# One order for all engines, worked out by a pass in time inside the kernel, for a convolution attention with two feed-forward layers

## The chip, the cores and the metric

The kernel runs on one core of a Trainium2 chip. The metric is the device time of one execution in microseconds (us), the median of three runs.

## What is computed

`x` and `weight_gen` are float32, the four weight matrices float64, taken in as pairs of 32-bit words. Products are made in fp32r with split operands (a high part and a low part).

```python
# x (2, 4096, 192), weight_gen (2, 4096, 8, 7)
w = softmax(weight_gen, axis=-1)                 # over the 7 taps, per token and head
x = einsum('bshk,bskhg->bshg', w, windows of 7 rows of x, zeros before the first)
x = x.reshape(8192, 192)
h = x @ w_in1;  x = (h * cos(h)) @ w_out1        # w_in 192 x 2048, w_out 2048 x 192
h = x @ w_in2;  x = maximum(0.01 * h, h) @ w_out2
```

## The kernel before

Tokens are cut into 16 blocks of 512 (4 rows of the sequence on each of 128 partitions). A block passes through three stages:

- Attention (`attention_ops`, L158 to L177): on VectorE (DVE), seven taps, each a product of a window of `xt` with a broadcast softmax weight and an add into `xa`, 14 instructions for a whole block; for blocks 0 and 1 the last quarter of the tokens goes to GpSimd (POOL) (`SPLIT`). Then TensorE (PE) transposes the block (`turn_ops`, six transposes) and the operands `xhi`, `xlo`, `xrh`, `xrl` are made from PSUM.
- Layer 1 and layer 2 (m = 0 and 1), each 16 chunks of 128 hidden columns. A chunk has five matmuls into a PSUM bank `h` (`hidden`, L358), the activation, and five matmuls into the two accumulators of its stream (`project`, L370 to L374). Layer 1's activation: ScalarE (ACT) makes the number of turns (L564), DVE the angle (L565), ACT the sine (L574), DVE the product (L575), ACT the high part `hi` (L251), POOL the low part `lo` (L254). Layer 2's: two Prelu on ACT (L569, L578) and `lo` on POOL.
- After a block's last chunk, `take` copies the sums out of PSUM (`om` by DVE, L385); they become layer 2's operands (`x2_ops`) or, transposed, the output (`result_ops`).

The weights come in as 32 units (two layers, four groups of four chunks, units a, r, 0 and 2) and are converted from float64 words by ACT (L232, L243, L251), POOL (clamp L233, add L246, low parts L254) and DVE (L236, L240). Low and high parts of the rest rows `r` are placed by DMA for the groups in `SPD`, by copies for the other two.

The 512 chunks stand in one list `seq`, taken in turn from two streams of blocks. By this list block 0 begins at chunk 0, block 1 at 7, block (1,0) of layer 2 has chunks 32 to 56, block 2 begins at 59, block 4 at 91; later each stream needs 32 places of the list for a block. Chunks 408, 440 and 472 are the last of blocks 13, 14 and 15 of layer 1.

The order on each engine is written out: for each place in the list the loop at the end emits the first activation step of this chunk, the second of the chunk before, the split of the one before that, and the projection of the chunk four places back (`LAG`); then the side work put down for this place: conversions at the places in `CONV_AT`, softmax by `softmax_at`, a block's attention over the 20 places before its turn (`attention_at`), and loads. All DMAs go through SyncE's queue. Every engine runs its instructions in the order in which they are emitted. Four PSUM banks `ps` are shared by `h` and the transposes.

## Time and profile before

| | |
|---|---|
| median of three runs | 1368.27 us (1367.78 to 1368.75) |
| the profiled execution | 1368.45 us, span 1366.4 us |
| PE busy | 1246.2 us (91%) |
| DVE, ACT, POOL busy | 817.5 us (60%), 875.5 us (64%), 852.2 us (62%) |
| first matmul of a chunk | 39.28 us |
| mean granted TensorE clock | 0.978 of full speed |

A busy share is an average over stages that have different limits, so the profile is read by stretches of time, and in each stretch by what an engine waited for. A matmul's row lasts longer than the distance to the next one, since matmuls overlap; starts tell the pace.

### The profile page before, as it was taken

What the parts mean: (1) busy time and instruction counts of PE and PEld (TensorE: products, weight loads), DVE (VectorE), ACT (ScalarE), POOL (GpSimd) and SP (SyncE); (2) the same over time, 40 slices, a digit from 0 to 9 for tenths busy, and PEclk for the clock granted to TensorE, in tenths of its full rate; (3) what the DMA queues carried; (4) which work ended last, traced back from release to release, by engine and by line L of the source; (5) the groups of instructions that cost most, each with busy time, mean ns of one, the idle gap of its engine ahead of it and who ended that gap; (6) DMA issues with size and microseconds to landing.
All of it is one profiled execution on the core that took longest, in us unless ns stands there. A gap on an engine that the chain in (4) does not pass through costs nothing.

```text
span 1366.4 us, 15432 instructions
## 1 busy us (share of the span) xinstructions
PE 1246.2 (91%) x5312; PEld 985.1 (72%) x5312; DVE 817.5 (60%) x1121; ACT 875.5 (64%) x1664; POOL 852.2 (62%) x680
## 2 busy tenths in 40 slices
PE   0667778799999999999999999999999999999998
PEld 0455556578787877878787777878787787888886
DVE  6997836778938386573838466473937557343100
ACT  2476666467765767666566766656676666676654
POOL 7888778456665655655556556555565665565654
PEclk9889889899999999999999999999999999999999
DMA  5323121101000001000000000000000000000000
GB/s 146 111 70 105 57 62 39 43 12 41 30 1 29 12 0 54 1 29 13 29 12 21 20 1 30 12 29 12 30 12 1 12 0 1 12 1 12 0 13 24
DMA packets 14398, 38.99 MB, mean 29 GB/s; under 512 B 1652, under 2 KB 7538, under 8 KB 14320
## 3 DMA queue, kind: packets, MB, share of 16 engines
q1 hardware_dynamic: 14320, 38.01, 8.5%
q8 instruction: 42, 0.69, 0.2%
q14 instruction: 36, 0.29, 0.1%
HBM read 30.13 MB, written 6.29 MB: 27 GB/s over the span
## 4 chain that ended last, share of the span: by engine, by line
PE 52%; DVE 19%; POOL 12%; issue 12%; ACT 2%; DMA 2%; SPq 0%; POOLq 0%; DVEq 0%; ACTq 0%
PE h L358 25%; POOL lo L254 9%; DVE xa L167 3%; DVE pr L165 3%; PE acc1m L374 3%; PE acc1r L373 3%; PE acc1r L372 3%; PE acc1m L370 3%; PE acc1m L371 3%; PE acc0r L373 3%; PE acc0m L374 2%; PE acc0m L371 2%; PE acc0m L370 2%; PE acc0r L372 2%; DVE g L565 2%
## 5 line engine op out<-in xcount | busy, mean ns | idle before, releaser
L254 POOL TENSOR_TENSOR lo<-g,hi 128x512 fp32r<-128x512 f32 x512 | 711.4, 1407 | 464.8 <-ACT hi L251 407.9
L565 DVE SCALAR_TENSOR_TENSOR g<-g,h 128x512 f32<-128x512 int32 x256 | 174.0, 681 | 239.8 <-POOL lo L254 147.8
L574 ACT ACTIVATE g<-g 128x512 f32<-128x512 f32 x256 | 161.3, 631 | 203.6 <-DVE g L565 202.7
L575 DVE TENSOR_TENSOR g<-h,g 128x512 f32<-128x512 f32 x256 | 175.7, 687 | 100.7 <-ACT g L574 100.0
L251 ACT ACTIVATE hi<-g 128x512 fp32r<-128x512 f32 x256 | 161.4, 631 | 42.4 <-DVE g L575 41.4
L564 ACT ACTIVATE g<-h 128x512 int32<-128x512 f32 x256 | 150.9, 591 | 58.2 <-PE h L358 56.2
L569 ACT ACTIVATE g<-h 128x512 f32<-128x512 f32 x256 | 151.7, 593 | 56.3 <-PE h L358 53.3
L578 ACT ACTIVATE hi<-h 128x512 fp32r<-128x512 f32 x256 | 151.9, 594 | 7.1 <-PE acc1r L372 0.3
L165 DVE TENSOR_TENSOR pr<-xt,smw 128x768 f32<-128x768 f32 (+1 forms) x96 | 132.2, 1377 | 1.4
L358 PE MATMUL h<-x0hi,ihi 128*128 128x512 f32 x256 | 106.9, 418 | 22.0 <-DVE g L575 17.6
L373 PE MATMUL acc0r<-lo,or 128*128 128x512 f32 x256 | 106.2, 415 | 19.6 <-POOL lo L254 19.6
L358 PE MATMUL h<-x1hi,ihi 128*128 128x512 f32 x256 | 105.4, 412 | 14.1 <-ACT hi L578 10.4
L370 PE MATMUL acc0m<-hi,ohi 128*128 128x512 f32 x256 | 103.6, 405 | 10.5 <-ACT g L574 7.3
L358 PE MATMUL h<-x1lo,ihi 128*128 128x512 f32 x256 | 101.5, 396 | 2.3 <-POOL x1lo L397 2.3
L358 PE MATMUL h<-x1rh,r 128*128 128x512 f32 x256 | 101.7, 397 | 2.0 <-ACT x1rh L218 2.0
L358 PE MATMUL h<-x1rl,r 128*128 128x512 f32 x256 | 101.6, 397 | 1.8 <-DVE x1rl L219 1.8
L358 PE MATMUL h<-x0hi,ilo 128*128 128x512 f32 x256 | 101.7, 397 | 1.6 <-POOL ilo L254 1.6
L167 DVE TENSOR_TENSOR xa<-xa,pr 128x768 f32<-128x768 f32 (+1 forms) x80 | 102.6, 1283 | 0.6
L358 PE MATMUL h<-x0lo,ihi 128*128 128x512 f32 x256 | 101.7, 398 | 1.3 <-DVE x0lo L198 1.3
L358 PE MATMUL h<-x0rh,r 128*128 128x512 f32 x256 | 102.0, 399 | 0.9 <-ACT x0rh L218 0.9
L372 PE MATMUL acc0r<-hi,or 128*128 128x512 f32 x256 | 101.6, 397 | 0.7
L358 PE MATMUL h<-x0rl,r 128*128 128x512 f32 x256 | 101.5, 397 | 0.0
(230 smaller groups left out, 2435.9 us busy)
## 6 DMA issues: line engine op xcount, KB each, us to landing
xt<-in_x SPq DMA_DIRECT2D x14, 960.0 KB, 4.7
wo<-in_moe_w_out SPq DMA_DIRECT2D x16, 384.0 KB, 3.2
out<-osb SPq DMA_DIRECT2D x16, 384.0 KB, 2.3
wa<-in_moe_w_in SPq DMA_DIRECT2D x8, 512.0 KB, 4.7
wr<-in_moe_w_in SPq DMA_DIRECT2D x16, 128.0 KB, 2.8
smw<-in_weight_gen SPq DMA_DIRECT2D x3, 448.0 KB, 5.4
xt<-in_x SPq DMA_DIRECT2D x1, 768.0 KB, 11.0
r<-whi SPq DMA_DIRECT2D x12, 64.0 KB, 2.9
```

Source lines behind the costliest of these rows:

```text
L165: eng.tensor_tensor(out=pr, in0=window(k), in1=weight(k), op=ALU.mult)
L251: nc.scalar.activation(out=hi, in_=v, func=AF.Copy)
L254: nc.gpsimd.tensor_tensor(out=lo, in0=v, in1=hi.bitcast(F32), op=ALU.subtract)
L358: nc.tensor.matmul(h, w[:, c], v, start=i == 0, stop=i == len(terms) - 1)
L370: nc.tensor.matmul(am, ohi, ghi, start=first, stop=False)
L372: nc.tensor.matmul(ar, orr, ghi, start=first, stop=False)
L373: nc.tensor.matmul(ar, orr, glo, start=False, stop=last)
L565: nc.vector.scalar_tensor_tensor(out=g, in0=k, scalar=-2 * math.pi, in1=h, op0=ALU.mult, op1=ALU.add)
L569: nc.scalar.activation(out=g, in_=h, func=AF.Prelu, alpha=0.01)
L574: nc.scalar.activation(out=g, in_=g, func=AF.Sin, bias=math.pi / 2)
L575: nc.vector.tensor_tensor(out=g, in0=h, in1=g, op=ALU.mult)
L578: nc.scalar.activation(out=ghi, in_=h, func=AF.Prelu, alpha=0.01)
```

## The change

The loop over places, `CONV_AT`, `PRE`, `LAG` and the helpers around them go. Every piece of work is now declared as an operation with a due time (in places of the list), its planned duration on each engine that may run it, what it reads and writes, and the buffers that it uses. `Plan.emit` then goes through time once: of all operations whose inputs are planned to be done and whose buffers are free, it takes, for the engine that can start first, the one with the smallest due time among those that can start within 0.12 us, puts it on that engine, and emits it. A second engine for an operation is taken only while the first is busy, and counts as 2 places later. A load is not taken before the plan's PE has come to 16 places ahead of its due time. The planned durations are fixed numbers in the code; a duration in brackets is multiplied by 1.35 when the plan's POOL is busy.

With it come: the `lo` split, the high part of layer 1, the clamp, the copies and low parts of the weights and some copies out of PSUM may go to DVE as a second engine; `h` may hold three of the four PSUM banks; six buffers `g` for seven; the taps run from the last to the first; only block 0 has a quarter on POOL; all `r` groups are placed by DMA. The list of chunks, the matmuls and the arithmetic are the same.

```diff
-SPD = {"03r", "01r", "13r", "12r", "00r", "02r"}
...
+class Buf:
+    def __init__(self, make, tag, cap, extra=(), line=None):
+        self.make, self.tags, self.tile = make, [(tag, cap), *extra], None
+        self.line = line
...
+class Plan:
+    HOP = 0.08
+    SLACK = 0.35
+    NEAR = 0.12
+    ELSE = 2.0
+    AHEAD = 16.0
+    SHARED = 1.35
...
+    def emit(self):
+        free = dict.fromkeys(("PE", "ACT", "DVE", "POOL", "SP"), 0.0)
+        wire = 0.0
+        self.at = -16.0
+        slots = {}
+        ready = [o for o in self.ops if not o.deps]
+        log = []
+        def start_of(o, e):
+            t = max(o.ready + (self.SLACK if e == "PE" else 0.0), free[e])
+            if e == "SP" and o.due > self.at + self.AHEAD:
+                return None
+            for b in o.bufs:
+                if not b.held:
+                    if b.line and self.lines[b.line][0] is not b:
+                        return None
+                    for tag, cap in b.tags:
+                        s = slots.setdefault(tag, [0.0] * cap)
+                        if not s:
+                            return None
+                        t = max(t, min(s))
+            return t
+        left = len(self.ops)
+        while left:
+            best = None
+            for e in free:
+                at = []
+                for o in ready:
+                    if e in o.cost:
+                        t = start_of(o, e)
+                        if t is not None:
+                            main = next(iter(o.cost))
+                            wait = 0.0 if e == main else self.ELSE
+                            if wait and free[main] <= t + self.NEAR:
+                                continue
+                            at.append((t, o.due + wait, o))
+                if at:
+                    t0 = min(a[0] for a in at)
+                    t, _, o = min((a for a in at if a[0] <= t0 + self.NEAR), key=lambda a: a[1])
+                    if best is None or t < best[0]:
+                        best = t, e, o
+            assert best
+            t, e, o = best
+            cost = o.cost[e]
+            if isinstance(cost, tuple):
+                cost = cost[0] * (self.SHARED if free["POOL"] > t + 0.2 else 1.0)
+            for b in o.bufs:
+                if not b.held:
+                    if b.line:
+                        self.lines[b.line].pop(0)
+                    for tag, _ in b.tags:
+                        slots[tag].remove(min(slots[tag]))
+                    b.held = True
+            free[e] = t + cost
+            o.end = t + cost
+            if e == "SP":
+                free[e] = t + 0.45
+                wire = max(wire, t) + cost
+                o.end = wire + 1.9
+            if e == "PE":
+                self.at = max(self.at, o.due)
+            o.fn(e)
+            log.append((t, e, o))
+            left -= 1
+            ready.remove(o)
+            for b in o.bufs:
+                b.users -= 1
+                b.end = max(b.end, o.end)
+                if not b.users:
+                    for tag, _ in b.tags:
+                        slots[tag].append(b.end)
+            for n in o.next:
+                n.ready = max(n.ready, o.end + self.HOP)
+                n.deps -= 1
+                if not n.deps:
+                    ready.append(n)
+        self.log = log
...
-    LAG = 4
-    STAGGER = 6
-    SMG = 4 * Q
-    RAW = 2
-    GBUFS = 7
-    PBUFS = 4
-    WA = 3
     GAP = 3
     TURN = 8
-    CONV_AT = [0, 2, 3, 3, 4, 5, 8, 8, 9, 12, 13, 13, 16, 20]
-    CONV_AT += [21, 22, 24, 26, 27, 28, 30, 32, 34, 36, 38, 40, 42, 44, 47, 50]
-    SPLIT = {0: 3, 1: 3, 2: 4}
-    PRE = [2,4,5,3,5,6,8,7,7,7]
+    STAGGER = 6
+    SPLIT = {0: 3}
+    PACE = {0: 0.5, 1: 0.9}
+    MM = 0.2275
+    GROUPS = [(0, 4), (4, 16), (16, 32), (32, 48), (48, 64)]
...
+    def temp(shape, tag, cap, name, dt=F32, line=None):
+        return Buf(lambda: work.tile(shape, dt, tag=tag, bufs=cap, name=name), tag, cap, line=line or tag)
+    def bank(name, kind):
+        return Buf(lambda: ps.tile([P, T], F32, tag="ps", name=name), "ps", 4, [kind])
...
+        op(due, {"SP": 0.55 * (Q + HALO - own)}, body, (), [("xt", b, 1)], [t])
...
+        parts = [(0, SPLIT.get(b, Q), "DVE"), (SPLIT.get(b, Q), Q, "POOL")]
+        last = begins - 2
+        pace = PACE.get(b, 2.6)
...
+            for i, k in enumerate(reversed(range(K))):
+                reads = [ksm, ("xt", b, 1)]
+                if q0 + k < own:
+                    reads += [("xt", b, 0, j) for j in ("z", *range(B))]
+                due = last - (K - i) * pace
+                cost = (0.1 + 0.2 * n,) if e0 == "DVE" else 0.25 + 0.6 * n
...
+                op(due, {e0: cost}, product, reads, [kp], [xt, smw, pr])
...
+                    op(due + 0.5 * pace, {e0: cost}, add, [kp, ka], [ka], [xa, pr])
...
+                main, rest = cost, cost
+                if e0 == "DVE":
+                    main, rest = (cost[0] * 0.75,), (0.5 if n == Q else 1.4,)
+                op(due + 0.4 * pace, {e0: main}, add_main, [kp, ka], [("xam", b, q0)], [xa, pr])
+                op(due + 0.6 * pace, {e0: rest}, add_rest, [kp, ka], [("xbr", b, q0)], [xa, pr, xb])
...
+            op(due - 4.4, {"ACT": 0.18 + 0.48 * w}, size, kr, [kt], [raw, t])
+            op(due - 4, {"POOL": 0.12 + 0.5 * w, "DVE": (0.12 + 0.35 * w,)}, clamp, [kt], [kt], [t])
+            op(due - 3.4, {"DVE": (0.12 + 0.35 * w,)}, shift, [kt], [kt], [t])
+            op(due - 2.8, {"DVE": (0.12 + 0.56 * w,)}, merge, [kt, *kr], [kt], [t, raw])
+            op(due - 3.2, {"ACT": 0.18 + 0.47 * w}, low, kr, [kv], [raw, v])
+            op(due - 2, {"POOL": 0.17 + 1.12 * w}, add, [kt, kv], [kv], [t, v])
...
+                    op(due - 1.6, {"ACT": 0.18 + 0.46 * w2, "DVE": (0.12 + 0.5 * w2,)},
+                       lambda e, h=h, t=t, c=c: copy(e, h, t().bitcast(F32)[c]), [kt], [(k, "hi", j)], [t])
+                    op(due - 0.9, {"POOL": 0.27 + 1.05 * w2, "DVE": (0.12 + 0.7 * w2,)},
+                       lambda e, h=h, l=l, v=v, c=c: minus(e, l, v().bitcast(F32)[c], h),
+                       [kv, (k, "hi", j)], [(k, "lo", j)], [v])
...
+            hi = temp([P, half], "whi", 2, f"whi{n}", F32R)
+            lo = temp([P, half], "wlo", 2, f"wlo{n}", F32R)
+            op(due - 1.6, {"ACT": 0.42, "DVE": (0.4,)}, lambda e, hi=hi, t=t: copy(e, hi(), t().bitcast(F32)), [kt], [(k, "whi")], [t, hi])
+            op(due - 0.9, {"POOL": 0.75, "DVE": (0.42,)}, lambda e, hi=hi, lo=lo, v=v: minus(e, lo(), v().bitcast(F32), hi()),
+               [kv, (k, "whi")], [(k, "wlo")], [v, hi, lo])
+            for j in range(2):
+                c = slice(j * half, (j + 1) * half)
+                r = slice(j * R, (j + 1) * R)
+                for name, src, rows in (("hi", hi, slice(0, R)), ("lo", lo, slice(R, P))):
+                    op(due, {"SP": 0.4}, lambda e, src=src, rows=rows, c=c, r=r: nc.sync.dma_start(
+                        out=ir[rows, c].bitcast(F32), in_=src()[r].bitcast(F32)), [(k, f"w{name}")], [(k, name, j)], [src])
+    RAW, WA, WN = 2, 3, 3
...
+        h = bank(f"h{m}_{b}_{f}", ("hq", 3))
+        g = temp([P, T], "g", 6, f"g_{pos}", line=f"g{st}")
+        ghi = temp([P, T], "hi", 4, f"hi_{pos}", F32R, f"hi{st}")
+        glo = temp([P, T], "lo", 4, f"lo_{pos}", F32R, f"lo{st}")
...
+        op(pos, {"PE": 5 * MM}, hidden, reads + [("order", st)], [kh, ("order", st)], [h, hi, lo, rh, rl])
...
+            op(pos + 0.5, {"ACT": 0.58}, turns, [kh], [kg], [h, g])
+            op(pos + 0.8, {"DVE": 0.67}, angle, [kh, kg], [kg], [h, g])
+            op(pos + 1.1, {"ACT": 0.62}, sine, [kg], [kg], [g])
+            op(pos + 1.4, {"DVE": 0.67}, times, [kh, kg], [kg], [h, g])
+            op(pos + 1.7, {"ACT": 0.62, "DVE": (0.6,)}, lambda e: copy(e, ghi(), g()), [kg], [khi], [g, ghi])
+        else:
+            op(pos + 0.6, {"ACT": 0.58}, lambda e: nc.scalar.activation(
+                out=g(), in_=h(), func=AF.Prelu, alpha=0.01), [kh], [kg], [h, g])
+            op(pos + 1.0, {"ACT": 0.58}, lambda e: nc.scalar.activation(
+                out=ghi(), in_=h(), func=AF.Prelu, alpha=0.01), [kh], [khi], [h, ghi])
+        op(pos + 2.0, {"POOL": 1.35, "DVE": (0.75,)}, lambda e: minus(e, glo(), g(), ghi()), [kg, khi], [klo], [g, ghi, glo])
...
+        op(pos + 2.5, {"PE": 3 * MM}, project_hi, [khi, *ws] + ([] if first else [ka]), [ka], [ghi, am, ar])
+        op(pos + 2.9, {"PE": 2 * MM}, project_lo, [khi, klo, ka] + ([] if first else [kb]), [kb], [ghi, glo, am, ar])
...
+    tops = {b: begin[0, b] for b in range(NB)}
+    for s0, s1 in GROUPS:
+        b = s0 // Q
+        softmax(s0, s1, tops[b] - 2 - (K + 1) * PACE.get(b, 2.6))
+    for b in range(NB):
+        x_load(b, tops[b] - 6 - K * PACE.get(b, 2.6))
+    for m, g in sorted(((m, g) for m in range(2) for g in range(NG)), key=lambda k: need[k[0], k[1] * GF]):
+        weights(m, g)
+    placed = set()
+    for pos, (st, m, b, f) in enumerate(seq):
+        if f == 0 and m == 0:
+            attention(b, tops[b])
+        chunk(pos, st, m, b, f)
+    LAST_PLAN.append(plan)
     with tc.manual_schedule():
+        plan.emit()
...
-    for pos in range(len(seq) + LAG):
-        for step, late in ((reduce, 0), (activate, 1), (part, 2)):
-            if 0 <= pos - late < len(seq):
-                step(pos - late)
-        if pos >= LAG:
-            st, m, b, f = seq[pos - LAG]
-            project(st, m, b, f, *live.pop(pos - LAG))
-            if f == NF - 1:
-                take(st, m, b)
-                if m == 0:
-                    spread(max(pos + 1, begin[1, b] - 4), x2_ops(b))
-                else:
-                    spread(pos + 2, result_ops(b))
-        while side.get(pos):
-            side[pos].pop(0)()
-    for pos in sorted(side):
-        while side[pos]:
-            side[pos].pop(0)()
```

## Rows read from the trace of the kernel before

**Rows 1.** The page's head: span, then busy time (share) and instructions.
```profile
span 1366.4 us, 15432 instructions
PE 1246.2 (91%) x5312; PEld 985.1 (72%) x5312; DVE 817.5 (60%) x1121; ACT 875.5 (64%) x1664; POOL 852.2 (62%) x680
```
**Rows 2.** Stretches: length, busy us (instructions) by engine, granted clock, DMA share, GB/s.
```profile
39.30:151.10 111.80, 81.06 (x283) 58.18 (x284) 97.21 (x140) 71.82 (x148) 92.36 (x93) 0.91 0.27 83
151.10:268.20 117.10, 92.11 (x340) 69.24 (x339) 74.09 (x109) 67.85 (x141) 84.74 (x80) 0.85 0.17 53
...
425.20:503.40 78.20, 76.42 (x333) 60.48 (x332) 47.20 (x63) 51.01 (x97) 46.20 (x34) 1.00 0.05 19
...
1202.70:1275.10 72.40, 72.40 (x324) 59.92 (x323) 26.35 (x40) 49.25 (x92) 43.48 (x34) 1.00 0.02 6
```
**Rows 3.** Timeline of DVE (start, duration, what): the copy that ends a block.
```profile
268.16 0.68 DVE L385 COPY om<-acc1m 128x512 f32<-128x512 f32 x1
...
1130.62 0.68 DVE L385 COPY om<-acc0m 128x512 f32<-128x512 f32 x1
...
1275.14 0.69 DVE L385 COPY om<-acc0m 128x512 f32<-128x512 f32 x1 [7.43 <-PE acc0m L374]
```
**Rows 4.** Timeline of PE: the first and the last of 96 matmuls, then transposes.
```profile
699.64 0.39 PE L358 MATMUL h<-x0rl,r 128*128 128x512 f32 x1
...
721.17 0.39 PE L374 MATMUL acc1m<-lo,ohi 128*128 128x512 f32 x1
721.40 0.60 PE L195 MATMUL tm<-ident,xa 128*128 128x128 f32 x4
721.76 0.48 PE L358 MATMUL h<-x0hi,ihi 128*128 128x512 f32 x1
```
**Rows 5.** Timeline of all engines during attention; in brackets the idle time before, and releaser.
```profile
415.66 5.22 POOL L254 TENSOR_TENSOR lo<-g,hi 128x512 fp32r<-128x512 f32 x3 [2.61 <-ACT hi L251]
415.78 1.98 DVE L165 TENSOR_TENSOR pr<-xt,smw 128x768 f32<-128x768 f32 x1
...
422.32 0.63 ACT L574 ACTIVATE g<-g 128x512 f32<-128x512 f32 x1 [4.28 <-DVE g L565]
...
423.68 0.94 DVE L165 TENSOR_TENSOR pr<-xt,smw 128x768 f32<-128x768 f32 x1
...
425.97 0.47 PE L370 MATMUL acc0m<-hi,ohi 128*128 128x512 f32 x1 [0.73 <-ACT g L574]
```
**Rows 6.** Timeline of the start: first tap, first matmul of a chunk.
```profile
9.57 0.76 DVE L158 TENSOR_TENSOR xa<-xt,smw 128x576 f32<-128x576 f32 x1 [4.08 <-DMA xt<-in_x]
...
39.28 0.79 PE L358 MATMUL h<-x0hi,ihi 128*128 128x512 f32 x1 [2.90 <-ACT x0hi L197]
```
**Rows 7.** Early stretch, groups (count, busy us, mean ns); `lo` of the span (min/median/max ns); longest wait.
```profile
L254 POOL TENSOR_TENSOR lo<-g,hi 128x512 fp32r<-128x512 f32 x59 | 85.3, 1458 | 16.9 <-ACT hi L578 11.0 <-ACT hi L251 5.8
L565 DVE SCALAR_TENSOR_TENSOR g<-g,h 128x512 f32<-128x512 int32 x34 | 22.6, 675 | 0.1
L575 DVE TENSOR_TENSOR g<-h,g 128x512 f32<-128x512 f32 x33 | 22.1, 678 | 1.5 <-ACT g L574 1.5
L165 DVE TENSOR_TENSOR pr<-xt,smw 128x768 f32<-128x768 f32 x13 | 19.2, 1474 | 0.2
...
L254 POOL TENSOR_TENSOR lo<-g,hi x512: 1262/1294/2103, 53.7 to 1356.0; 128x512 fp32r<-128x512 f32 x171
...
DVE wt L236 <- POOL wt L233: 22.9, 8, 6.9
```
**Rows 8.** Groups of DVE's attention between 430 and 1130 us, nine blocks.
```profile
L165 DVE TENSOR_TENSOR pr<-xt,smw 128x768 f32<-128x768 f32 x54 | 79.1, 1464 | 1.0
L167 DVE TENSOR_TENSOR xa<-xa,pr 128x768 f32<-128x768 f32 x44 | 59.6, 1354 | 0.3
L171 DVE TENSOR_TENSOR xa<-xa,pr 128x512 f32<-128x512 f32 x9 | 15.9, 1766 | 0.3
...
L158 DVE TENSOR_TENSOR xa<-xt,smw 128x768 f32<-128x768 f32 x9 | 8.6, 959 | 9.6 <-PE tm L195 9.6
L174 DVE TENSOR_TENSOR xb<-xa,pr 128x256 f32<-128x256 f32 x9 | 8.2, 916 | 0.0
```

More of the change, by code (lines that the diff above doesn't have):

```diff
@@ L22, with __call__, __init__ @@
 MOST = (2 - 2.0**-3 - 2.0**-23) * 2.0**16
-SPD = {"03r", "01r", "13r", "12r", "00r", "02r"}
+class Buf:
+    def __init__(self, make, tag, cap, extra=(), line=None):
+        self.make, self.tags, self.tile = make, [(tag, cap), *extra], None
+        self.line = line
+        self.users, self.end, self.held = 0, 0.0, False
+    def __call__(self):
+        if self.tile is None:
+            self.tile = self.make()
+        return self.tile
+class Op:
+    def __init__(self, due, cost, fn, deps, bufs):
+        self.due, self.cost, self.fn, self.bufs = due, cost, fn, bufs
+        self.deps, self.next, self.ready, self.end = len(deps), [], 0.0, None
+        for d in deps:
+            d.next.append(self)
@@ L27, in conv_attention_moe_moe @@
+LAST_PLAN = []
 @with_exitstack
@@ L350, in hidden @@
-    def hidden(m, b, f):
-        hi, lo, rh, rl = x_of[m, b]
-        assert {(m, f // GF, "a"), (m, f // GF, "r")} <= ready
-        ihi, ilo, ir = W[m, f // GF][:3]
-        c = slice((f % GF) * P, (f % GF + 1) * P)
-        h = ps.tile([P, T], F32, tag="ps", name=f"h{m}_{b}_{f}")
-        terms = [(ihi, hi), (ilo, hi), (ihi, lo), (ir, rh), (ir, rl)]
-        for i, (w, v) in enumerate(terms):
-            nc.tensor.matmul(h, w[:, c], v, start=i == 0, stop=i == len(terms) - 1)
-        return h
@@ new lines, in conv_attention_moe_moe, with copy @@
+    plan = Plan()
+    op = plan.op
+    eng = {"DVE": nc.vector, "POOL": nc.gpsimd}
+    def temp(shape, tag, cap, name, dt=F32, line=None):
+        return Buf(lambda: work.tile(shape, dt, tag=tag, bufs=cap, name=name), tag, cap, line=line or tag)
+    def bank(name, kind):
+        return Buf(lambda: ps.tile([P, T], F32, tag="ps", name=name), "ps", 4, [kind])
+    def copy(e, out, in_):
+        if e == "ACT":
+            nc.scalar.activation(out=out, in_=in_, func=AF.Copy)
+        else:
+            eng[e].tensor_copy(out=out, in_=in_)
@@ new lines, in conv_attention_moe_moe, with x_load, body, zero @@
+    xt_of = {}
+    def x_load(b, due):
+        t = Buf(lambda: xin.tile([P, (Q + HALO) * D], F32, tag="xt", name=f"xt{b}"), "xt", 2, line="xt")
+        first = Q * b - HALO
+        own = max(-first, 0)
+        xt_of[b] = t, own
+        def body(e):
+            nc.sync.dma_start(out=t()[:, own * D :], in_=xf[:, (first + own) * D : (first + Q + HALO) * D])
+        op(due, {"SP": 0.55 * (Q + HALO - own)}, body, (), [("xt", b, 1)], [t])
+        if not own:
+            return
+        def zero(e):
+            for j in range(B):
+                nc.gpsimd.memset(t()[j * PPB : j * PPB + 1, : own * D], 0.0)
+        def halo(e, j):
+            a = j * PPB
+            nc.sync.dma_start(
+                out=t()[a + 1 : a + PPB, : own * D], in_=xf[a : a + PPB - 1, (NS - own) * D :]
+            )
+        op(due, {"POOL": 0.4 * own}, zero, (), [("xt", b, 0, "z")], [t])
+        for j in range(B):
+            op(due, {"SP": 0.3 * own}, lambda e, j=j: halo(e, j), (), [("xt", b, 0, j)], [t])
@@ new lines, in place @@
+    def place(m, b, due, key, src, v):
+        rh, rl = x_of[m, b][2:]
+        halves = (slice(0, R), slice(0, HT)), (slice(R, P), slice(HT, T))
+        for i, (p, c) in enumerate(halves):
+            op(due, {"ACT": 0.39}, lambda e, p=p, c=c: copy(e, rh()[p, c], v()[p]), [key], [("rh", m, b, i)], [rh, src])
+            op(due + 0.2, {"DVE": 0.42}, lambda e, p=p, c=c: minus(e, rl()[p, c], v()[p], rh()[p, c]),
+               [key, ("rh", m, b, i)], [("rl", m, b, i)], [rh, rl, src])
+        for i, ((p, c), (p2, _)) in enumerate(zip(halves, reversed(halves))):
+            op(due + 0.4, {"ACT": 0.39}, lambda e, p=p, p2=p2, c=c: copy(e, rh()[p2, c], v()[p]), [key], [("rh", m, b, 2 + i)], [rh, src])
+            op(due + 0.6, {"DVE": (0.3,)}, lambda e, p=p, p2=p2, c=c: copy(e, rl()[p2, c], rl()[p, c].bitcast(F32)),
+               [("rl", m, b, i)], [("rl", m, b, 2 + i)], [rl])
@@ new lines, in conv_attention_moe_moe @@
+    op(-90, {"POOL": 1.0}, constants, (), ["ident"])
+    plan.writers["order", 0] = plan.writers["order", 1] = []
+    tops = {b: begin[0, b] for b in range(NB)}
[7 more added lines that the diff above has]
+    placed = set()
```

678 lines of the change are left out of this document (294 added, 384 removed).

## Prediction

> **What bounds the kernel now.** I read the page's head first: TensorE (PE) is busy 91% of the span and no other engine reaches 65% [rows 1]. A busy share says little about stages, so the second view is the table of stretches [rows 2]. The cuts are the moments at which VectorE (DVE) copies a finished block out of PSUM [rows 3], because these stand at known places in the list of 512 chunks: 268.16 us is the end of chunk 56, 1130.62 that of chunk 408, 1275.14 that of chunk 472. Three regimes come out.
>
> In the last, without attention, 64 chunks take 1275.14 - 1130.62 = 144.5 us, or 72.3 us for 32. A matmul there starts every (721.17 - 699.64)/95 = 0.2266 us [rows 4]; 320 of them make 72.5 us. Nothing is lost: PE is the bound.
>
> In the middle, 352 chunks take 1130.62 - 268.16 = 862.5 us, 78.4 us for 32. The four transposes of a block hold PE 0.36 us [rows 4], so all six some 0.6 us; the rest of the excess, 78.4 - 72.3 - 0.6 = 5.5 us in each of 11 periods, about 60 us in all, is PE standing still. The stretch rows show the same: 76.4 of 78.2 us busy with 333 matmuls, against 324 in 72.4 us later [rows 2]. Where it goes is seen in one attack of attention: three taps of 1.9 to 2.0 us run on DVE beside a GpSimd (POOL) that is in `lo`, the sine on ScalarE (ACT) waits 4.28 us for the DVE step behind them, and PE's projection then waits for that sine [rows 5].
>
> At the start, the first `h` matmul begins at 39.28 us [rows 6], and 56 chunks (plus the four still in flight) are through at 268.16 us, 229 us later; 60 chunks at PE's pace are 136 us. Here 93 us are lost. DVE is busy 97.2 of 111.8 us and then 74.1 of 117.1, POOL 92.4 and 84.7 [rows 2]: PE waits for them, and the granted clock of 0.85 to 0.91 is a consequence of its pauses. So PE bounds the end, DVE with POOL the beginning, and single DVE steps in the wrong place the middle.
>
> **The change, early stretch.** The chunk list, the matmuls and the arithmetic stay; what moves is the order on each engine. From 39.3 to 268.2 us POOL is busy 177.1 us and DVE 171.3 [rows 2]. If the order alone were perfect, the 229 us could shrink to 177, a gain of 52; that is the upper end.
> - Taken off POOL: a quarter of block 1's attention (13 operations, about 0.8 us each beside DVE: 10 us) and those `lo` that the planner gives to DVE. There are 59 in this stretch at 1.458 us [rows 7]; I take 15 of them, 22 us, since the rule wants DVE free while POOL is not. POOL: 177 - 32 = 145.
> - On DVE: block 4's attention, not due before chunk 91, may only be loaded when the plan's PE has come to chunk 51 (due 67, less 16); some half of its 14 steps at 1.47 us [rows 7] falls behind chunk 56, -10 us. Block 1's taps, a third wider, cost 13 x 0.2 = +3, the 15 `lo` about 0.9 us each, +13 (nearest row: the 128x512 add, 0.68 alone by its share of the 768 tap, 1.77 as measured [rows 8]). DVE: 171 - 10 + 3 + 13 = 177.
> - In-order waits go: DVE stood 22.9 us behind POOL's clamp of the weights [rows 7], because the three steps of a conversion were put down together. The planner starts a step only when its input is due.
> - So DVE is next, with 177 us of work. It held 87% in the first stretch; at 88%, 177 takes 201 us, 28 less than 229.
> - The start itself lies in front: attention of block 0 begins at 9.57 us [rows 6], and the planner puts two output-weight conversions (four DVE steps, 3.5 us) and the second softmax group behind or ahead of it; I expect the first `h` near 31 us, but DVE's backlog then takes most of that, so it stands for 2 us. Copies of weights that leave ACT for DVE give back 5. Together 28 + 2 - 5 = 25 us; bounds 0 and 52.
>
> **The change, middle.** The 14 attention steps of a block cost DVE (79.1 + 59.6 + 8.6 + 15.9 + 8.2)/9 = 19.0 us [rows 8]. The planner counts 0.9 us for a tap and 1.215 when its POOL is still busy, 12.0 or 16.2 us for the 14. POOL is busy some 60% of these stretches [rows 2], so its mean is 14.5 us: it believes DVE 4.5 us freer per block than it is. It fills every DVE gap with a tap as soon as `xt` is there, so for some 24 us its DVE is full, and on the chip the chain step behind falls late by up to 4.5 us. What covers it: three `h` banks let PE be one chunk ahead, 2.3 us. PE then loses 4.5 - 2.3 = 2.2 us per block in place of 5.5, and 3.3 x 11 = 36 us are won. If nothing covers it, 1.0 x 11 = 11; if everything does, 60. Against it stands the part that may go to either engine: if a third of the 16 `hi` copies in a period leaves a busy ACT for DVE, where it meets POOL, and each costs PE 0.2 us, that is 1.0 x 11 = 11 us. I take 36 - 11 = 25.
>
> **The rest.** Moved DMAs: each load is put on SyncE's queue when its buffer is free by plan; the two `r` groups now placed by DMA add 8 small ones, behind nothing urgent. The fourth PSUM bank that `h` gives up, six `g` buffers for seven: with the cosine a chunk holds its bank for its matmuls, 1.13 us, two ACT steps of about 0.6 [rows 5] and two DVE steps of 0.68 [rows 7], 3.7 us plus hand-overs, and less without, while three banks turn round in 6.8; cover is there, and if it were not the middle's 2.2 us would return to 5.5. Tail: nothing but PE's pace, 0, within 2.
>
> Sum: the profiled execution took 1368.45 us (span 1366.4, [rows 1]), 0.2 us over the median of the three runs, and 1368.3 - 25 - 25 = 1318 us.
>
> **A rule that speaks against it.** The rows show that a DVE tap takes 0.94 us beside an idle POOL and 1.98 beside `lo` [rows 5], while `lo` goes from its shortest, 1.26, to a mean of 1.458 in the early stretch [rows 7]. The Trainium skill, SBUF — State Buffer, section "SBUF: two separate sides", says that DVE steps with two SBUF inputs and POOL steps that read SBUF take turns for one pair of ports, whole instructions at a time. By that rule the sum would be about 1399 us, the third case below; what it does to this kernel is worked out there from rows alone.
>
> **The rivals.**
> 1. *The plan holds as it is priced.* DVE and POOL take turns well, the middle runs at 72.3 + 0.6 us and the early stretch wins 40 of 52: 1368 - 40 - 50 = 1278 us. For it: the last regime shows PE at its pace with the same chain of steps. Against: the tap's price.
> 2. *Nothing changes.* The new waits are as long as the old: engines run in order as before, and the early stretch is bound by work that the order doesn't remove. 1366 to 1371 us.
> 3. *Taps wait out POOL, slower.* Place: DVE, while a plan-full stretch of attention runs. If taps and `lo` exclude each other, then each of the 12 taps packed densely takes 1.94 us, 12 x 1.94 + 1.8 + 0.9 = 26.0 us a block; late by 26.0 - 14.5 - 2.3 = 9.2 us against 5.5 now: 11 x 3.7 = +41. Early, POOL's unstretched work (177 x 1.26/1.458 = 153) and DVE's other steps (171 less 45 for the two chunk steps, which read PSUM [rows 7]; 126 x 0.94/1.47, some 80 unstretched) share one resource: 233 of 229 us are full already, and only the reliefs count, 10 us. 1368 + 41 - 10 = 1399 us. It decides from a mean tap of about 1.75 us on (where 14 steps' lateness eats 5.5 and the early 25/11); measured are 1.35 to 1.46 [rows 8], with less dense packing. Against it too: 153 + 80 us did fit, and PE's waits in [rows 5] are under a microsecond each.
>
> **How the numbers follow.** Forecast 0.56 (its own range 1290 to 1350), rival 1 0.20, rival 2 0.06, rival 3 0.15; 0.03 lies between 1350 and 1366, counted as faster. Faster by over 0.2% (about what a measurement of this kernel can tell from no change): 0.56 + 0.20 + 0.02 = 0.78; within it 0.06; slower 0.16. The likeliest time is 1318. For 8 in 10 the range runs from 1270, below rival 1's time by what its two halves may be off, to 1374, just past rival 2; rival 3 stays out.
>
> **What would show it.** Right: the copy of block (1,0) out of PSUM at 243 us instead of 268, the first `h` near 31; periods of 75 to 76 us; some tens of `lo` on DVE; the wait for POOL's clamp gone. Wrong: periods over 78 us with ACT's sine or PE waiting for the DVE step behind taps (rival 3), or `lo` on DVE at 1.9 us; periods of 73 and an early stretch under 200 us (rival 1). A PE that waits for a bank of `h` would mean that the three banks, which I cost at nothing, are the bound. DMA would be my blind spot: a tap order that waits for `xt` on DVE.

## The result, and the profile after

The changed kernel takes 1335.63 us (1334.98 to 1336.07) against 1368.51 us for the kernel before in the same comparison: a ratio of 0.9759 (95% interval 0.9742 to 0.9776), 33 us won where 50 were forecast. The profiled execution has a span of 1333.5 us, 33 less than in [rows 1]. The head of its page, to be read beside [rows 1] (busy us, share, instructions):

```profile
span 1333.5 us, 15316 instructions
PE 1231.4 (92%) x5312; PEld 980.6 (74%) x5312; DVE 1031.3 (77%) x1314; ACT 841.0 (63%) x1583; POOL 653.5 (49%) x502
```

Some 200 us of work have left POOL, and DVE has gained 214. The copies of finished blocks out of PSUM cut the span at the same places of the list as in [rows 3]: the end of block (1,0), of (0,13) and of (0,15). The timeline of DVE shows the three, with two ends of blocks between them:

```profile
223.01 0.69 DVE L225 COPY om<-acc1m 128x512 f32<-128x512 f32 x1
...
618.98 0.69 DVE L225 COPY om<-acc0m 128x512 f32<-128x512 f32 x1
...
697.12 0.69 DVE L225 COPY om<-acc0m 128x512 f32<-128x512 f32 x1
...
1089.60 0.69 DVE L225 COPY om<-acc0m 128x512 f32<-128x512 f32 x1
...
1241.23 0.69 DVE L225 COPY om<-acc0m 128x512 f32<-128x512 f32 x1 [1.43 <-PE acc0m L632]
```

The stretches between them, with the columns of [rows 2] (length, busy us and instructions by engine, granted clock, DMA share, GB/s):

```profile
28.50:223.00 194.50, 159.26 (x608) 117.46 (x606) 186.97 (x237) 134.47 (x276) 148.69 (x133) 0.94 0.28 84
223.00:1089.60 866.60, 834.86 (x3652) 669.23 (x3653) 705.42 (x893) 554.08 (x1025) 375.31 (x257) 1.00 0.06 19
1089.60:1241.20 151.60, 148.33 (x657) 120.97 (x656) 102.53 (x133) 97.71 (x179) 57.05 (x42) 1.00 0.02 6
```

So the whole gain lies in the first stretch. The two later stretches of the kernel before, for comparison:

```profile
268.20:1130.60 862.40, 841.43 (x3663) 668.83 (x3663) 548.73 (x734) 575.99 (x1081) 511.61 (x364) 1.00 0.05 18
1130.60:1275.10 144.50, 143.32 (x635) 117.01 (x635) 61.81 (x93) 99.40 (x186) 86.10 (x67) 1.00 0.02 6
```

The same table for all kernels of this study follows. "PE still" is worked out from the starts of all matmuls in the 352 chunks: how far each start lies behind the one before beyond PE's pace (0.2267 us after a matmul, 0.09 after a transpose), summed over the gaps above 0.12 us; how rows are merged for it moves a figure by up to some 2 us. All but the last two columns come from the profiled execution; each ratio is to the kernel before, run beside it (medians of 1367.9 to 1369.3 us).

| kernel | to the end of (1,0) | 352 chunks | PE still in these | next 64 chunks | median, us | ratio to before (95%) |
|---|---|---|---|---|---|---|
| before | 268.2 | 862.5 | 34.8 | 144.5 | 1368.5 | |
| after | 223.0 | 866.6 | 44.2 | 151.6 | 1335.63 | 0.9759 (0.9742 to 0.9776) |
| e1_hi_act | 226.7 | 864.5 | 40.1 | 150.7 | 1335.45 | 0.9754 (0.9740 to 0.9769) |
| e2_lo_pool | 228.3 | 884.6 | 59.9 | 153.1 | 1360.86 | 0.9940 (0.9925 to 0.9955) |
| e3_first_engine | 250.2 | 868.9 | 52.3 | 152.7 | 1363.15 | 0.9957 (0.9942 to 0.9971) |
| e4_tap_price | 226.3 | 859.4 | 37.2 | 149.9 | 1329.81 | 0.9714 (0.9698 to 0.9730) |
| e5_slack | 237.0 | 870.4 | 48.6 | 153.8 | 1354.00 | 0.9890 (0.9874 to 0.9907) |
| e6_four_banks | 224.9 | 863.5 | 42.8 | 151.7 | 1336.28 | 0.9766 (0.9750 to 0.9781) |
| e7_two_taps | 221.5 | 830.4 | 13.2 | 148.7 | 1295.78 | 0.9469 (0.9455 to 0.9483) |
| e8_prices | 225.1 | 852.7 | 33.4 | 149.9 | 1321.14 | 0.9654 (0.9640 to 0.9669) |
| e9_one_pair | 275.9 | 828.5 | 12.9 | 146.6 | 1344.88 | 0.9827 (0.9811 to 0.9844) |
| e10_early_loads | 228.2 | 874.4 | 51.7 | 151.6 | 1348.25 | 0.9856 (0.9841 to 0.9871) |
| e11_two_stages | 218.8 | 832.2 | 13.5 | 146.4 | 1291.54 | 0.9433 (0.9418 to 0.9449) |

From before to after the early stretch gives 45.2 us, the 352 chunks lose 4.1, the next 64 lose 7.1, and the rest 1.0.

These differences hold some work that only moved across a cut. A cut is a copy of one stream's sums, and PE need not be at the same matmul there. By their starts, PE has begun 612 instructions at the first cut where it had begun 628 before; the 352 chunks hold 3652 for 3663, the next 64 hold 656 for 634, the rest 392 for 387 (the rows above, which count what touches a stretch, show the same to one or two). All of the difference is matmuls, at 0.2267 us each: 3.6 and 2.5 us of work less, then 5.0 and 1.1 us more. At equal work the early stretch gives 41.6 us, the middle loses 6.6, the next 64 chunks lose 2.1, and the rest is level.

**Early.** PE's first `h` comes at 28.45 us instead of 39.28 [rows 6], and from there DVE is busy 187.0 of 194.5 us, 96%, against 75% from 39.30 to 268.20 [rows 2]. The 22.9 us for which DVE stood behind POOL's clamp [rows 7] have shrunk to waits of under a microsecond each. POOL is busy 149 us there, and 18 `lo` have gone to DVE (groups from 0 to 223 us: count, busy us, mean ns):

```profile
28.45 0.78 PE L576 MATMUL h<-x0hi,ihi 128*128 128x512 f32 x1
```
```profile
L228 DVE TENSOR_TENSOR lo<-g,hi 128x512 fp32r<-128x512 f32 x18 | 22.5, 1265 | 0.3 <-ACT hi L223 0.2
```

**Middle.** Two blocks end at 618.98 and 697.12 us: a period of 78.1 us, no shorter than the 78.2 of [rows 2]. What PE waits for there is read from the waits of PE from 223 to 1090 us (total, times, longest):

```profile
PE acc0m L626 <- DVE hi L225: 20.0, 17, 2.6
PE acc0m L626 <- ACT hi L223: 4.5, 10, 1.0
```

and one of them from the timeline of all engines:

```profile
698.84 1.91 DVE L390 TENSOR_TENSOR xa<-xa,pr 128x768 f32<-128x768 f32 x1
...
699.88 2.01 POOL L228 TENSOR_TENSOR lo<-g,hi 128x512 fp32r<-128x512 f32 x1
...
700.78 1.94 DVE L383 TENSOR_TENSOR pr<-xt,smw 128x768 f32<-128x768 f32 x1
...
702.74 0.69 DVE L595 SCALAR_TENSOR_TENSOR g<-g,h 128x512 f32<-128x512 int32 x1
...
703.47 0.63 ACT L600 ACTIVATE g<-g 128x512 f32<-128x512 f32 x1 [2.10 <-DVE g L595]
...
704.28 0.68 DVE L603 TENSOR_TENSOR g<-h,g 128x512 f32<-128x512 f32 x1
...
705.06 0.43 DVE L225 CAST hi<-g 128x512 fp32r<-128x512 f32 x1
...
705.54 0.50 PE L626 MATMUL acc0m<-hi,ohi 128*128 128x512 f32 x1 [2.12 <-DVE hi L225]
```

It is the picture of [rows 5] with one more step: two taps of 1.9 us beside POOL's subtractions make the angle late, ACT waits 2.10 us for it, the product and `hi` follow, and PE stands 2.12 us. The groups from 400 to 1080 us:

```profile
L228 DVE TENSOR_TENSOR lo<-g,hi 128x512 fp32r<-128x512 f32 x93 | 121.6, 1308 | 65.1 <-ACT hi L613 60.8 <-ACT hi L223 1.6
L383 DVE TENSOR_TENSOR pr<-xt,smw 128x768 f32<-128x768 f32 x51 | 72.8, 1428 | 0.6
L390 DVE TENSOR_TENSOR xa<-xa,pr 128x768 f32<-128x768 f32 x42 | 59.5, 1416 | 0.6
L225 DVE CAST hi<-g 128x512 fp32r<-128x512 f32 x33 | 14.1, 427 | 3.9
```

**Late.** Of the 7.1 us, 5.0 are the 22 matmuls more between the cuts; some 2 us are left in which PE stands. One statement on the kernel before doesn't hold here: its section with a fixed order covers the start alone, and in the loop the order of emission is not the order on the engines. Its timeline shows block 15's attention ahead of its turn and, but for one product at 1064.25, done in one go of 28 us, while the transposes come 50 us later; by the order of emission it would be spread over the 20 places, some 46 us, ahead of them:

```profile
1113.00 0.96 DVE L158 TENSOR_TENSOR xa<-xt,smw 128x768 f32<-128x768 f32 x1 [1.06 <-PE tm L195]
...
1139.21 1.77 DVE L171 TENSOR_TENSOR xa<-xa,pr 128x512 f32<-128x512 f32 x1
...
1189.58 0.60 PE L195 MATMUL tm<-ident,xa 128*128 128x128 f32 x4
```

So of block 15's 14 steps, 6 (8.1 us) lay behind the cut at 1130.62 [rows 3]. In the changed kernel 10 (13.0 us) lie behind the cut at 1089.60, the last at 1119.2. That these four steps cost the 2 us is not shown: the fastest kernel below has 9 steps there and takes 146.4 us.

### The profile page after: what moved, and what is told of

Read it like the earlier page. It is cut to its first block, busy times and chain, and to the rows that moved or that the text cites. A ratio compares the mean times of both kernels' runs of the same rounds, so it can differ in the third digit from the quotient of the medians.

```text
span 1333.5 us, 15316 instructions
## 1 busy us (share of the span) xinstructions
PE 1231.4 (92%) x5312; PEld 980.6 (74%) x5312; DVE 1031.3 (77%) x1314; ACT 841.0 (63%) x1583; POOL 653.5 (49%) x502
## 4 chain that ended last, share of the span: by engine, by line
PE 49%; DVE 33%; ACT 7%; issue 6%; POOL 1%; DMA 1%; DVEq 0%; SPq 0%; ACTq 0%; POOLq 0%
PE h L576 24%; DVE xa L390 6%; DVE g L603 5%; DVE g L595 5%; DVE pr L383 4%; DVE lo L228 3%; PE acc0m L626 3%; PE acc1m L626 3%; PE acc1r L631 3%; PE acc1r L628 3%; PE acc1m L627 3%; PE acc1m L632 3%; PE acc0r L628 2%; PE acc0m L627 2%; PE acc0r L631 2%
## 5 line engine op out<-in xcount | busy, mean ns | idle before, releaser
L228 POOL TENSOR_TENSOR lo<-g,hi 128x512 fp32r<-128x512 f32 x362 | 520.9, 1444 | 632.3 <-ACT hi L223 345.9
L228 DVE TENSOR_TENSOR lo<-g,hi 128x512 fp32r<-128x512 f32 x150 | 192.9, 1288 | 95.0 <-ACT hi L613 89.6
L223 ACT ACTIVATE hi<-g 128x512 fp32r<-128x512 f32 x211 | 133.0, 631 | 74.5 <-DVE g L603 69.8
L613 ACT ACTIVATE hi<-h 128x512 fp32r<-128x512 f32 x256 | 150.7, 589 | 0.1
L383 DVE TENSOR_TENSOR pr<-xt,smw 128x768 f32<-128x768 f32 (+1 forms) x96 | 131.9, 1374 | 1.1
L631 PE MATMUL acc1r<-lo,or 128*128 128x512 f32 x256 | 101.7, 397 | 9.7 <-DVE lo L228 5.0
L390 DVE TENSOR_TENSOR xa<-xa,pr 128x768 f32<-128x768 f32 (+1 forms) x80 | 106.6, 1333 | 0.9
L576 PE MATMUL h<-x0hi,ihi 128*128 128x512 f32 x256 | 102.6, 401 | 2.8 <-DVE g L603 2.6
L626 PE MATMUL acc1m<-hi,ohi 128*128 128x512 f32 x256 | 102.6, 401 | 1.7 <-ACT hi L613 1.7
```

Source lines behind the costliest of these rows:

```text
L228: eng[e].tensor_tensor(out=out, in0=a, in1=b.bitcast(F32), op=ALU.subtract)
L383: eng[e].tensor_tensor(out=pr(), in0=window(k), in1=weight(k), op=ALU.mult)
L390: eng[e].tensor_tensor(out=a, in0=a, in1=pr(), op=ALU.add)
L576: nc.tensor.matmul(h(), w[:, c], v(), start=i == 0, stop=i == len(terms) - 1)
L626: nc.tensor.matmul(am(), ohi[:, f % GF, :], ghi(), start=first, stop=False)
L631: nc.tensor.matmul(ar(), orr[:, f % GF, :], glo(), start=False, stop=last)
```

## The experiments

Three theories were set against each other for the middle. **T**: taps are planned too short, so DVE is late against the plan. **H**: `hi` on DVE is what PE waits for, and without that choice the wait goes. **L**: hand-overs come late in general, and slack for PE in the plan would cover it. For the first stretch the question was whether the order wins or the choice of engine. All edits are against the changed kernel.

**The parts of the change.** `hi` on ACT alone (e1), `lo` on POOL alone (e2), no choice at all (e3):

```diff
-            op(pos + 1.7, {"ACT": 0.62, "DVE": (0.6,)}, lambda e: copy(e, ghi(), g()), [kg], [khi], [g, ghi])
+            op(pos + 1.7, {"ACT": 0.62}, lambda e: copy(e, ghi(), g()), [kg], [khi], [g, ghi])
```

> The changed kernel with layer 1's high part `hi` of a chunk on ACT alone. Theory H (the plan prices a `hi` on DVE at 0.6 to 0.81 us and puts it behind attention steps; PE waits 22.7 us for it between 223 and 1090 us, all else follows from that): the waits of PE for `hi` fall to those of a `hi` on ACT, under 10 us, and the time to 1312 to 1322 us. Rival T (DVE is late because a tap takes 1.42 us where 0.9 to 1.2 are planned, and `hi` is only the step that shows it): the lateness comes back at the sine or the product, and the time stays within 5 us of 1336. Rival A (ACT becomes too full): slower than 1340.

Nothing changed in the time: 1335.45 us. The wait moved. PE's waits from 227 to 1091 us:

```profile
PE acc0m L626 <- ACT hi L223: 26.5, 36, 1.9
PE h L576 <- DVE g L603: 2.2, 4, 0.7
```

26.5 us for ACT's `hi` in place of 20.0 for DVE's and 4.5 for ACT's. The last step before PE was only the messenger; H falls.

```diff
-        op(pos + 2.0, {"POOL": 1.35, "DVE": (0.75,)}, lambda e: minus(e, glo(), g(), ghi()), [kg, khi], [klo], [g, ghi, glo])
+        op(pos + 2.0, {"POOL": 1.35}, lambda e: minus(e, glo(), g(), ghi()), [kg, khi], [klo], [g, ghi, glo])
```

> The changed kernel with a chunk's `lo` on POOL alone (150 of them ran on DVE at 1.29 us, planned 0.75 to 1.01). Theory R (taking `lo` off POOL is what won the early stretch): block (1,0) ends 8 to 20 us later than at 223 us, the whole 1340 to 1355 us. Rival D (a `lo` on DVE costs as much of the shared time as it saves, and burdens the engine that the middle waits for): the early end moves by less than 5 us and the middle gains 5 to 20 us, 1316 to 1330 us.

25 us lost: 5 early and 18 in the 352 chunks. Neither theory fits: R wanted 8 to 20 us early, and D a gain in the middle. The choice of `lo` is worth having with these prices, and most of its worth lies in the middle, though a `lo` on DVE takes 1.3 us where 0.75 (1.01 beside POOL) is planned.

```diff
+        cost = dict(list(cost.items())[:1])
         o = Op(due, cost, fn, deps, list(dict.fromkeys(bufs)))
```

> The changed kernel with every operation on its first engine only: the order alone, without the choice. If the early gain comes from the order and from putting attention off, block (1,0) ends within 223 to 238 us and the whole stays under 1345 us; if it comes from the choice, block (1,0) ends after 245 us and the whole is 1350 us or more. In the middle theory H expects PE's waits for `hi` on DVE (22.7 us) to go; rival T expects them elsewhere.

The first stretch ends at 250.24 us:

```profile
250.24 0.68 DVE L226 COPY om<-acc1m 128x512 f32<-128x512 f32 x1
```

So the order, with the smaller edits that came with it, wins 268.2 - 250.2 = 18 us early, and the choice of engine 250.2 - 223.0 = 27, or some 23 at equal work (PE has begun 634 instructions at this cut, 612 in the changed kernel). The profiled execution of e3 is its slowest, 3.2 us over its median, so the two parts are about equal. With e1 (3.7) and e2 (5.3), some 11 to 18 us remain for the other choices (clamps, copies and low parts of the weights and of layer 2's operands), by difference and if the parts add. In the 352 chunks no choice (868.9) does better than all choices but `lo` (884.6): there the parts don't add.

**The middle's cause.** Taps with the durations that the trace shows (e4), slack for PE (e5), the fourth bank for `h` (e6), and fewer taps (e7, which leaves out five of the seven taps of blocks 4 to 15 and so computes something else):

```diff
-                cost = (0.1 + 0.2 * n,) if e0 == "DVE" else 0.25 + 0.6 * n
+                cost = (0.1 + 0.21 * n, 2.05) if e0 == "DVE" else 0.25 + 0.6 * n
...
-                    main, rest = (cost[0] * 0.75,), (0.5 if n == Q else 1.4,)
+                    main, rest = (cost[0] * 0.75, 2.5), (0.5 if n == Q else 1.4, 1.8)
...
-                cost = cost[0] * (self.SHARED if free["POOL"] > t + 0.2 else 1.0)
+                cost = cost[0] * ((cost[1] if len(cost) > 1 else self.SHARED) if free["POOL"] > t + 0.2 else 1.0)
```

> The changed kernel with the taps of attention planned at what the trace shows: 0.94 us, and 1.93 beside a busy POOL, in place of 0.9 and 1.215; nothing else. Theory T (the tap's price is what makes DVE late): the middle loses less, 1308 to 1322 us. Theory H: `hi` still goes to DVE at its old price, the time moves by less than 8 us either way.

PE stands 7.0 us less in the 352 chunks, and the time falls by 5.8 us (1329.62 to 1330.02, clear of the changed kernel's range). T is right in its sign, but its 1308 to 1322 us were missed, and H's condition (less than 8 us) holds for the time as well; it is e1 that speaks against H. With the price alone 37 us of standing still remain.

```diff
-    SLACK = 0.35
+    SLACK = 1.2
```

> The changed kernel with PE's work planned 1.2 us after its inputs are ready by plan, in place of 0.35; nothing else. In the runs so far PE stood still 37 to 60 us in the middle, always in front of a projection that waits for layer 1's `hi`, whichever engine made it. Theory L (the plan puts a projection directly behind its input, so every lateness of the chain reaches PE): more slack hides it, PE stands still under 25 us in the middle, 1314 to 1326 us. Rival B (PSUM banks bound how far PE can run ahead, so slack is only PE waiting by plan): 1336 us or more. Rival T (DVE has too little time while taps run, whatever the order): within 5 us of 1336.

18 us slower, as rival B has it; 14 of them lie early, and why there was not followed up. In the middle PE now waits for the product that frees a bank, 2.6 us in all in the changed kernel (PE's waits from 237 to 1107 us):

```profile
PE h L576 <- DVE g L603: 18.9, 17, 2.6
```

L falls: with more planned slack PE stands 48.6 us instead of 44.2, now before `h`, where it waits for a bank.

```diff
-        h = bank(f"h{m}_{b}_{f}", ("hq", 3))
+        h = bank(f"h{m}_{b}_{f}", ("hq", 4))
```

> The changed kernel with `h` allowed in all four PSUM banks instead of three; nothing else. I costed the fourth bank at nothing. If three banks bound PE's lead, the middle gains 8 to 25 us: 1310 to 1328. If not, within 4 us of 1336; if `h` then keeps the transposes waiting, up to 10 us slower.

1336.28 us (1334.23 to 1339.07): no difference. The cost of nothing that the prediction put on the three banks was right.

```diff
-            for i, k in enumerate(reversed(range(K))):
+            for i, k in enumerate(reversed(range(K)) if b < 4 else (K - 1, 0)):
```

> The changed kernel with five of the seven taps left out for blocks 4 to 15 (4 DVE steps in place of 14), so the middle has little attention; the first four blocks are whole. Theory T (taps beside POOL make the chain late): PE's standing still in the middle falls from 44 to under 15 us and the last two blocks lose their 7 us, 1298 to 1310 us. If the plan's tight projections were enough for the loss by themselves (theory L without taps), over 25 us remain, 1318 us or more.

PE's standing still falls from 44.2 to 13.2 us and the 352 chunks to 830.4:

```profile
221.50:1051.90 830.40, 820.92 (x3653) 670.24 (x3653) 578.79 (x799) 566.50 (x1033) 323.21 (x236) 1.00 0.06 20
```

Without most of the taps the loss in the middle is gone, and so is some of DVE's load; that the work of the taps need not cost it is shown by the last run below, which has all of them. In the next 64 chunks 2.9 of the 7.1 us come back.

**Prices or a shared resource.** e8 adds to e4 new prices for a `lo` and a `hi` on DVE: 0.68 and 0.33 us, and 1.9 times as much (1.29 and 0.63) while the plan's POOL is busy:

> The changed kernel with the measured prices for everything that showed a wrong one: taps as in the run before (0.94 and 1.93), `lo` on DVE 0.68 and 1.29 beside POOL (0.75 and 1.01 before), `hi` on DVE 0.33 and 0.63 (0.6 and 0.81). Theory T: the plan now sees DVE's load, and gives `lo` to it less often; 3 to 10 us under the 1329.8 of the tap price alone. If prices past the tap's don't matter: within 3 us of it.

1321.14 us: another 8.7 us, and PE stands 33.4 us. The choice is now made less often where it hurts (groups from 400 us to the cut; 93 at 1308 ns in the changed kernel):

```profile
L228 DVE TENSOR_TENSOR lo<-g,hi 128x512 fp32r<-128x512 f32 x81 | 87.9, 1085 | 30.2 <-ACT hi L613 26.8 <-issue 0.9
```

e9 leaves the factor out. The steps in brackets, to which two steps of the softmax are added, and all of POOL's are planned as users of one resource, one after the other, each with its undisturbed duration:

```diff
+        def shares(o, e):
+            return e == "POOL" or e == "DVE" and isinstance(o.cost[e], tuple)
...
+            if shares(o, e):
+                t = max(t, pair)
...
-                cost = cost[0] * (self.SHARED if free["POOL"] > t + 0.2 else 1.0)
+                cost = cost[0]
...
+            if shares(o, e):
+                pair = t + cost
```

> The changed kernel whose plan treats POOL's steps and DVE's steps in brackets as one resource: none starts before the other engine's has ended, each at its undisturbed duration (tap 0.94, `lo` 0.68 on DVE and 1.28 on POOL, `hi` 0.33), in place of the factor 1.35. If the two engines really take turns, the plan now places every step where it will run, and DVE's attention and `lo` stand off each other: 1300 to 1316 us, PE still under 25 us in the middle. If they overlap in part (a sum of 106% of the time was read for 39 to 151 us of the kernel before), the plan is too slow and holds PE back: 1322 to 1345 us. No difference from the run with measured prices: 1318 to 1324.

It wins and loses. The whole time, 1344.88 us, falls where the expectation put a partial overlap (1322 to 1345), while PE stands 12.9 us in the middle, as expected if the engines take turns. The middle is the shortest of all, and the first stretch is worse than before:

```profile
275.93 0.69 DVE L233 COPY om<-acc1m 128x512 f32<-128x512 f32 x1
```
```profile
275.90:1104.50 828.60, 818.91 (x3651) 672.67 (x3651) 531.10 (x729) 566.20 (x1039) 502.12 (x365) 1.00 0.05 19
```

In that first stretch all 59 `lo` of `g` went back to POOL, as is to be expected of a plan in which both engines take turns, and PE stood waiting for POOL's `lo` (28 us in 14 waits; 11 us in the changed kernel), for attention (22 us in four waits) and once 13.4 us for a DMA that places a weight. The granted clock is 0.83 there, 0.94 in the changed kernel's first stretch. It isn't for want of a second engine alone: e3, which has none, is through at 250.2 us.

```profile
L236 POOL TENSOR_TENSOR lo<-g,hi 128x512 fp32r<-128x512 f32 x59 | 84.1, 1436 | 2.2 <-ACT hi L231 2.2
```

Another doubt was whether the rule that loads come at most 16 places ahead only puts attention off (e10):

```diff
-    AHEAD = 16.0
+    AHEAD = 48.0
```

> The changed kernel with loads allowed 48 places ahead of PE instead of 16, so attention of blocks 2 to 4 may run while the weights are converted, as it did before the change. If putting attention off is a large part of the early gain, block (1,0) ends 8 to 25 us later than at 223 us, and some 7 us come back in the last two blocks: 1334 to 1352 us in all. If not, (1,0) ends within 4 us of 223, and the whole is 1326 to 1336 us.

12.6 us slower, and the last 64 chunks take 151.6 us as before this edit, so the 7 us that were expected back there didn't come. The first stretch grows by 5.2 us, between the two expectations (within 4, and 8 to 25); putting attention off is worth at most that. That the 352 chunks grow by 7.8 us has no explanation from these runs.

**Both together.** e11 takes e8's prices until the plan's PE has come to chunk 56, and e9's shared resource from there (`lo` on POOL 1.35 us for the chunks before that, 1.28 after):

```diff
+        def shares(o, e):
+            return self.at >= 56 and (e == "POOL" or e == "DVE" and isinstance(o.cost[e], tuple))
...
+                late = self.at >= 56 or free["POOL"] <= t + 0.2
+                cost = cost[0] * (1.0 if late else cost[1] if len(cost) > 1 else self.SHARED)
```

> The changed kernel with the measured prices up to chunk 56 of the plan's PE, and from there on with POOL's and DVE's bracketed steps as one resource at their undisturbed durations. The run with measured prices had its first stretch at 225 us, the run with one resource its middle and end at 828.5 and 146.6 us. If the two halves are independent: 225 + 829 + 147 + 92 = 1293, 1286 to 1303 us, faster than every kernel so far; PE still under 20 us in the middle. If the fast middle of that run came from attention done ahead in its long first stretch, the middle is 845 us or more and the whole 1310 us or more.

1291.54 us (1289.61 to 1291.84), 44 us under the changed kernel and 5.7% under the one before: the fastest of all. Its head, its two later stretches, PE's only wait of size in the 352 chunks, and the groups from 400 to 1040 us:

```profile
span 1289.6 us, 15425 instructions
PE 1215.3 (94%) x5312; PEld 984.0 (76%) x5312; DVE 851.8 (66%) x1143; ACT 859.4 (67%) x1614; POOL 830.2 (64%) x642
```
```profile
218.80:1051.00 832.20, 823.61 (x3667) 675.70 (x3666) 569.39 (x771) 573.10 (x1056) 515.62 (x367) 1.00 0.06 20
1051.00:1197.40 146.40, 146.19 (x654) 120.54 (x653) 69.69 (x104) 99.77 (x181) 87.36 (x67) 1.00 0.02 6
```
```profile
PE acc0m L635 <- ACT hi L232: 7.0, 5, 2.4
```
```profile
L392 DVE TENSOR_TENSOR pr<-xt,smw 128x768 f32<-128x768 f32 x49 | 74.0, 1510 | 0.6
L399 DVE TENSOR_TENSOR xa<-xa,pr 128x768 f32<-128x768 f32 x40 | 51.6, 1290 | 0.3
L237 POOL TENSOR_TENSOR lo<-g,hi 128x512 fp32r<-128x512 f32 x273 | 375.5, 1394 | 244.1 <-ACT hi L232 178.4 <-DVE hi L234 19.3 <-ACT hi L622 17.9
```

The taps are no shorter than in the changed kernel (1.51 and 1.29 us against 1.43 and 1.42), and no `lo` of this stretch runs on DVE. That isn't it alone: e2 has no `lo` on DVE either and takes 884.6 us, and e3, with no `hi` there as well, 868.9. So with nearly the same split of work (12 `hi` on DVE in the 352 chunks; 47 in e2, none in e3) 37 to 52 us lie between a plan with the old prices and the factor 1.35 and one with measured durations that makes a step wait its turn. Nor was attention done ahead, as it was in e9 (122 of its steps into `pr` and `xa` in the 352 chunks): 157 of them lie here, 155 in the changed kernel. That the chain's DVE step is no longer put behind taps that end late fits this: ACT's waits for the angle fall from 161.1 us in the 352 chunks of the changed kernel to 96.6. (Alone they don't set PE's time: the kernel before has 172.0.) How much is the turn and how much the prices is not separated, since no kernel with measured prices and `lo` on POOL alone was run.

## Why the prediction was right, and where it missed

The forecast was 1318 us in a range of 1270 to 1374; 1335.63 lies in it, faster as forecast, with two thirds of the gain. The likeliest case came true in kind, but that the sum came so near is in part luck: its two halves were both mis-sized, in opposite ways, the early one by 20 us too little and the middle by 29 too much.

- **Early, -45 for -25.** Within the bounds (0 and 52). The first mis-sized term is the first `h`: 10.8 us earlier, counted as 2 since DVE's backlog would take the rest. It didn't: DVE is busy 19.1 of the 19.5 us ahead of the first `h`, so no backlog was left to take it. The second is DVE's fill: its work was under-estimated (187.0 us for 177), but it filled 96% of the stretch where 88% was taken, so the stretch took 194.5 us and not 201. The third is the copies of the weights given to DVE, +5 in the sum; the other choices together win some 11 to 18 (e3 less e1 and e2), so the sign was wrong. POOL at 145 us (measured 148.7) and the clamp's wait were right; 15 `lo` at 0.9 us were 18 at 1.27. Of the 45 us, 3.6 are matmuls that moved behind the cut.
- **Middle, +4 for -25.** The step that failed is "PE then loses 4.5 - 2.3 = 2.2 us per block in place of 5.5". Of the 5.5 us only 34.8/11 = 3.2 were PE standing still in gaps above 0.12 us; the rest is mostly the six transposes of a result, which the prediction left out, and smaller gaps. This alone takes 2.3 x 11 = 25 us, the whole forecast. Then the loss after is not 2.2 + 1.0 for `hi`, but 44.2/11 = 4.0: if the lateness of 4.5 us was right, which no run measures, the cover of 2.3 us from three banks wasn't there in full, and a fourth bank adds none (e6). The term for `hi` was no addend, since the wait moves to ACT without it (e1). Standing still grew by 9.4 us, 11 fewer matmuls between the cuts give 2.5 back, and the other 2.8 lie in smaller gaps and in the accuracy of the sum: +4.1. The mechanism, a plan whose taps are shorter than the chip's, was right but not the whole: without most taps the loss goes (e7), their right price wins 5.8 us of the time and all right prices 14.5 (e4, e8), yet these take only 10.8 of the 31 us of standing still that go without the taps; the rest went only where steps are planned in turn and `lo` is back on POOL (e9, e11).
- **Late, +7 for 0.** Some 5 of the 7.1 us are the 22 matmuls more between the cuts, so the 0 was off by about 2. The prediction's 144.5 us are not 64 chunks' full work: PE begins 634 instructions there, and 640 matmuls and 18 transposes belong to 64 chunks. Nor was the stretch without attention, since 6 steps of block 15 lie in it. Without most taps 2.9 us come back (e7); e11 takes 5.3 us less, 1.1 of them for 5 matmuls fewer.
- **Three banks, DMA and tail at nothing:** right (e6; no wait of DVE for `xt`, or of PE for any DMA, is seen in the changed kernel; 1.0 us in the tail).
- **Rival 3** ran from a mean tap of 1.75 us on; it stayed at 1.42 to 1.43, and the kernel came out faster. **Rival 1**'s middle (72.9 us per period) wasn't reached by any full kernel: e9 takes 828.5/11 = 75.3 and e11 832.2/11 = 75.7.
- Of "what would show it": the first `h`, the `lo` on DVE (150 in all) and the vanished wait for the clamp came, and the copy of block (1,0) at 223 us, 20 ahead of the 243 expected; periods of 75 to 76 us did not (78.1), and the sign given there for that, the sine waiting for the DVE step behind taps, is just what the timeline shows.

The rule that was weighed, that of the Trainium skill (SBUF — State Buffer, section "SBUF: two separate sides"), failed as a forecast of slower and proved its worth as a model for the plan: steps planned in turn, whole steps at a time, take PE's standing still in the middle from 44.2 to 12.9 us (e9; 33.4 with measured prices and factors in e8), though `lo` stays on POOL then as well. In the first stretch the same rule gave 275.9 us for 223.0. There the measurement decides against it as a plan; whether because steps overlap in part, or because without the choice of engine the load was badly placed, these runs don't separate.

## What to carry to other kernels

A static order is as good as its prices: read the duration of each step alone and beside its neighbour from a trace and put both in, and where two engines slow each other down, try planning them as one resource, stage by stage, before giving work to a second engine. Work given to a second engine won where engines are full and PE waits for them (the start: e3), and little where the trouble is the moment at which a step is due (the middle: 868.9 us without any, 866.6 with all). When a wait is the last link of a chain, removing that link shows only the next one; ask what was late first, and count how long the bound engine really stands still before counting how much of it can be won. And when stretches are cut at an event of one stream, count the work between the cuts before reading a difference as won or lost.
